# Sparse attention into a feed-forward block on one core: two score tiles, four query turns, two key turns and the last transposes put elsewhere in the order

## The chip, the cores and the metric

The kernel runs on one core of a Trainium2 chip. The metric is device time in microseconds for one execution; the median of four runs is compared. The core has five engines that run side by side, each through its own instructions in order: TensorE (PE in the profile; its weight loads are PEld), VectorE (DVE), ScalarE (ACT), GpSimd (POOL) and SyncE (SP, which here only issues DMAs). They wait for one another by semaphores.

## The reference

Inputs q, k, v are 4 batches x 8 heads x 768 rows x 64, in float32. Each query sees the keys less than 16 rows away, and one summary key and value for each of the 24 blocks of 32 rows: the maximum of the block's keys and the mean of its values. The outcome goes through a feed-forward block with a sigmoid-approximated gelu.

```python
k_sum = k.reshape(B, H, nb, block, D).max(axis=3)
v_sum = v.reshape(B, H, nb, block, D).mean(axis=3)
scores_l = scale * q @ k.T            # kept where |i - j| < 16
scores_s = scale * q @ k_sum.T + log(block)
a = softmax(concat([scores_l, scores_s]))
x = (a @ concat([v, v_sum]))          # heads side by side: 3072 x 512
h = x @ w_in                          # 512 x 2048
out = (h * sigmoid(1.702 * h)) @ w_out
```

## The kernel before

**Units.** Each of the 4 batches is cut into two halves of 384 rows; the eight halves are the units u = 0 to 7. Attention of a unit works on four pairs of heads, p = 0 to 3. In the names of the order tables a lower-case letter is a batch's first half and a capital its second half: `s2` is "scores of pair 2, first half", `S2` the same of the second half, `v1` / `V1` the values of pairs 2 and 3, `x1` / `X1` their transposition into the layout that the feed-forward reads, `t2` and `q2` the turning of the queries of pair 2.

**Attention of one pair.** `scores` (line 606) is 24 small matmuls on TensorE into a PSUM tile of two banks, one exponential on ACT and one multiplication by the mask on VectorE. `values` (616) is 24 matmuls for each pair, and `norm` (639) on VectorE. Then either `tx` (645) transposes with TensorE and a copy, or `dx` (653) with a transposing DMA on SP's queue. Keys and queries are turned by TensorE (`tk` 567, `tq1`, `q_turn` 434 with `q_copy` 443) in the first batches, and by transposing DMAs on SP's queue (`xk` 579, `xq` 587, with `rest_k` 593 on VectorE behind them) in the later ones. The turns of `tk` give VectorE a copy, a maximum, and the copies `key_halos` and `key_rows`.

**Feed-forward.** `ff_in` (658) makes 16 tiles of 128 hidden columns for a unit, each four matmuls of 384 columns and one gelu on ACT. For units 0 and 1 the output stage is `ff_out` (807): three row tiles (ms) in four parts each. For later batches the output stage is a Strassen-Winograd scheme over pairs of row tiles, class `Pair`: seven products p1 to p7 for each of the pairs a, b, c. Three of them accumulate onto one PSUM bank `x`, and between them ACT copies the bank out (`held`, 849), so that the next of them waits for that copy: p6, then p5, then p3. For the last batch the same scheme is used within `ff_in` too (`ff_in_pairs`, 700), with products M1 to M7 over weight sums and sums of the two units' x; six tiles of unit 6 are done plainly ahead of it, while the sums `t[0]` to `t[3]` are made on VectorE. They need the transposed x of both halves.

**PSUM.** Pool `pmm` (77) has four banks, for feed-forward products, turned queries, and the x of `tx`. Pool `psb` (76) has two tiles of two banks, for scores, turned keys, and values. A new tile waits until a bank of its pool is read out.

**Order.** Every engine's instructions keep the order in which the program writes them (class `_Ordered`; line 28 is that of every instruction in the profile). So the order around the change is written out by hand, in tables:
- `plan0` and `plan1` (1056 to 1060), read by `beside` (1064), put attention steps of the next unit behind the slots of `ff_out`. Slot -1 is ahead of the first output product. Behind `beside(1, -1)` the program issues the loads of the next q and k rows on POOL's queue.
- `todo` (1101) puts key turns, the copies `v_odd` and `value_rows` behind the hidden tiles of unit 1. `value_rows` sums v over blocks (TensorE, then VectorE) and issues on POOL's queue the DMAs that fill the halo and sum rows of `vw`, and further loads.
- `order` and `meets` (1129 to 1136), read by `attend` (1138), do the same for the output stages of batches 1 and 2, beside attention of batches 2 and 3. Behind the pair S3, `gelu_soon` has ACT load the gelu table.
- A product's store, where it has one, is issued on SP's queue when the product is written (`store`, 874): p3 and p4 of each pair store a row tile, before that batch's next entries of `meets`.

Of the kernel before, what the change touches and what calls it, by code (L numbers as in the profile page):

```python
# [35 lines left out]
def kernel(  # L36
# [239 lines left out]
    def copy(eng, out, in_):  # L276
        if eng is act:
            act.activation(out=out, in_=in_, func=ACT.Copy)
        elif eng == "dve_alone":

            dve.tensor_reduce(out=out, in_=in_.unsqueeze(len(in_.shape)), axis=AX.X, op=ALU.max)
        else:
            eng.tensor_copy(out=out, in_=in_)
# [94 lines left out]
    def at(ap, start, dims):  # L378
        a = ap[:, start:start + 1]
        return bass.AP(tensor=a.tensor, offset=a.offset, ap=[a.ap[0]] + dims)  # L380

    def flat_kx(p, s):
        return kx[p][s].rearrange("p t c -> p (t c)")
# [7 lines left out]
    def key_halos(p, s, eng=dve, j0=0):  # L391

        flat = flat_kx(p, s)
        b0 = max(j0, 1)
        o = 256 * j0
        eng.tensor_copy(out=at(flat, 256 * b0 + 96, [[256, NJ - b0], [1, 16]]),
                        in_=at(flat, 256 * b0 - 16, [[256, NJ - b0], [1, 16]]))
        eng.tensor_copy(out=at(flat, o + 128 + 48, [[256, NJ - 1 - j0], [1, 16]]),
                        in_=at(flat, o + 256, [[256, NJ - 1 - j0], [1, 16]]))
        eng.tensor_copy(out=at(flat, o + 128 + 32, [[256, NJ - j0], [-48, 2], [1, 16]]),  # L400
                        in_=at(flat, o + 48, [[256, NJ - j0], [144, 2], [1, 16]]))
# [159 lines left out]
    def trans(src):  # L561
        big = psb.tile([128, 2048], BF16, name="ps_t", tag="big")
        for j in range(NJ):
            pe.transpose(out=big[:, j * 128:(j + 1) * 128], in_=src[:, j], identity=ident)
        return big[:, 0:S]

    def tk(p, s):
        ps = trans(rows["k", 1][:, p].rearrange("p j h d -> p j (h d)"))
        copy(dve, at(flat_kx(p, s), 0, [[256, NJ], [192, 2], [1, 64]]),
             ps.rearrange("p (j e c) -> p j e c", e=2, c=64))  # L570
        ks = attp.tile([128, nb], BF16, name="ks", tag="ks")
        dve.tensor_reduce(out=ks, in_=ps.rearrange("p (n s) -> p n s", s=block),
                          axis=AX.X, op=ALU.max)
        key_halos(p, s)
        key_rows(p, s, ks)
# [124 lines left out]
    def ff_in_pairs(u, early):  # L700

        (b11, b21), (b12, b22) = xTT
        xs = castp2.tile([128, 4, 2, HALF], F16, name="xsum", tag="kb")
        t = [xs[:, m] for m in range(4)]
        big = [psb.tile([128, 1024], F32, name="pw_in", tag="big") for _ in range(2)]
        mm = [pmm.tile([128, 512], F32, name="px_in", tag="mm") for _ in range(4)]
        X, V = ([m[:, 0:HALF] for m in mm[n:n + 2]] for n in (0, 2))
        Y = [big[0][:, n:n + HALF] for n in (0, 512)]
        L = big[1][:, 0:HALF]

        def gelu(w, f, src):
            act.activation(out=gT[w % 2][:, f, :], in_=src, func=ACT.Gelu_apprx_sigmoid)

        def one(w, f, ps):
            for ko in range(KO):
                pe.matmul(out=ps, lhsT=w_in_sb[:, ko, f * 128:(f + 1) * 128], rhs=xT[w % 2][ko],
                          start=(ko == 0), stop=(ko == KO - 1))
            gelu(w, f, ps)

        def prod(ps, a, b, i, first=False):  # L720
            for k in range(2):
                pe.matmul(out=ps, lhsT=a[:, k, i], rhs=b[:, k], start=(first and k == 0),
                          stop=(k == 1), skip_group_check=True)

        ws = [wt["s"][:, n] for n in range(4)]
        hold = {}

        def f0(i):
            return 2 * (NI - WI + i)

        def M1(i):
            x = X[i % 2]
            prod(x, wt[0, 0], b11, i, True)
            dve.tensor_copy(out=Y[i % 2], in_=x)

        def M7(i):
            v = V[i % 2]
            prod(v, ws[2], t[2], i, True)
            hold[i] = attp.tile([128, HALF], F32, name="m7", tag="x2")
            copy(act, hold[i], v)  # L740

        def M6(i):
            x = X[i % 2]
            prod(x, ws[1], t[1], i)
            dve.tensor_add(V[i % 2], x, hold[i])

        def M2(i):
            y = Y[i % 2]
            prod(y, wt[0, 1], b21, i)
            gelu(u, f0(i), y)  # L750

        def M5(i):
            x = X[i % 2]
            prod(x, ws[0], t[0], i)
            hold[i, 2] = attp.tile([128, HALF], F32, name="c22", tag="a_sb")
            dve.tensor_add(hold[i, 2], x, hold[i])

        def M4(i):
            v = V[i % 2]
            prod(v, wt[1, 1], t[3], i)  # L760
            gelu(u, f0(i) + 1, v)
            gelu(u + 1, f0(i) + 1, hold[i, 2])

        def M3(i):
            x = X[i % 2]
            prod(x, ws[3], b22, i)
            gelu(u + 1, f0(i), x)

        n, rest = 2 * (NI - WI), list(range(2 * (NI - WI)))

        def plain():
            one(u + 1, rest.pop(0), L)

        for f, ps in zip(range(n), (Y[0], X[1], V[1], Y[1], L, X[1])):
            if f == n - 2:
                M1(0)
            one(u, f, ps)
        dve.tensor_sub(t[2], b22, b12)
        dve.tensor_add(t[1], t[2], b11)
        dve.tensor_sub(t[0], b12, b11)  # L780
        dve.tensor_sub(t[3], b21, t[1])
        M2(0)
        M7(0)
        plain()
        M6(0)
        for i in range(1, WI):
            M1(i)
            for f in (M7, M5) if i == 1 else (M5, M7):
                f(i if f is M7 else i - 1)
            M4(i - 1)  # L790
            M6(i)
            M3(i - 1)
            M2(i)
            plain()
            if i == 2:
                early(0, NI - WI)
        i = WI - 1
        M5(i)
        M4(i)
        early(NI - WI, NI)  # L800
        plain()
        M3(i)
        assert not rest
# [244 lines left out]
    for p in range(NP):  # L1048
# [7 lines left out]
    plan1 = {0: ["t0"], 1: ["t1"], 2: ["s0", "s1"], 4: ["t2"], 5: ["t3"],  # L1056
             6: ["v0", "s2", "s3"], 8: ["x0"], 9: ["v1", "S0", "S1"], 11: ["x1", "S2", "S3"]}

    plan0 = {-1: ["q0", "q1", "q2", "q3"], 1: ["s0", "s1"], 3: ["s2", "s3"], 6: ["v0", "v1"],
             9: ["x0"], 10: ["x1"]}  # L1060

    w51 = vw[1].rearrange("p (j e) h c -> p j e h c", e=2)
# [23 lines left out]
    for u in range(2):  # L1086
        todo = {}
        if u == 0:
            for p in range(NP):
                todo.setdefault(12 + p // 2, []).append(lambda p=p: cast_q(dve, p, 1))  # L1090
        else:
            def value_rows():
                vsum(1, range(NJ))
                block_sums()
                halo_dmas(w51, 0)
                sum_dmas(w51, 0)
                load_kc(2, range(6, H))
                load_vc(2)
                load_qc(2)

            todo = {0: [lambda: tk(0, 1)], 3: [lambda: tk(1, 1)], 5: [lambda: v_odd(1)],
                    6: [lambda: tk(2, 1)], 9: [value_rows], 11: [lambda: tk(3, 1)]}
            ff_in(u, range(3))
        for nt in range(0 if u else N0, NT):
            if u == 0 or nt > 2:
                ff_in(u, (nt,))
            for f in todo.get(nt, ()):
                f()
        exp_soon()
        if u == 0:  # L1110
            beside(1, -1)
            load_qc(1)
            load_kc(2, range(6))
        order = [(ms, part) for ms in range(JH) for part in range(4)]
        if u == 0:

            order = [(ms, part) for part in range(4) for ms in range(JH)]
        for i, (ms, part) in enumerate(order):
            ff_out(u, ms, part)
            beside(u + 1, i)  # L1120
            if u == 0 and i in (4, 7, 10):
                w_sums(i // 3 - 1)
            if u == 1 and i == 2:
                w_sums(3)
            if u == 1 and i == 3:
                for g in range(2):
                    xk(g, 2)
# [1 line left out]
    order = ["a7", "a2", "a6", "b1", "a5", "b7", "a3", "a4", "b6", "b2", "b5",  # L1129
             "c1", "b3", "c7", "c6", "c2", "c5", "b4", "c3", "c4"]  # L1130
    meets = {1: {"a7": ["s0", "s1"], "a5": ["s2", "s3"], "b6": ["v0", "v1"], "b5": ["x0"],
                 "c1": ["x1"], "b3": ["S0", "S1"], "c2": ["S2", "S3"],
                 "c4": ["V0", "V1", "X0", "X1"]},
             2: {"a7": ["s0", "s1"], "b1": ["s2", "s3"], "a4": ["v0", "v1"], "b2": ["x0"],
                 "b5": ["x1"], "c1": ["S0", "S1"], "c6": ["S2", "S3"], "c2": ["V0"],
                 "b4": ["X0"], "c3": ["V1", "X1"]}}

    def attend(b, what):
        half, i = int(what[0].isupper()), int(what[1])
# [10 lines left out]
    for b in range(1, B):  # L1150
        n, s = b + 1, (b + 1) % 2
# [97 lines left out]
```

## Time and profile before

| | us |
|---|---|
| median of 4 runs | 209.73 (209.48 to 210.36) |
| the profiled execution | 209.58 |
| its span, first to last instruction | 207.9 |
| TensorE busy | 198.4, 95% of the span |
| VectorE busy | 146.7, 71% |
| ScalarE busy | 124.1, 60% |
| GpSimd busy | 93.3, 45% |
| granted TensorE clock, mean | 0.997 |

The page of the profile gives busy time by engine, then the span in 40 slices of 5.2 us with a busy digit for each (9 is 90% or more). The chain of waits that ended last is 85% TensorE, 6% DMA and 4% VectorE; its largest links are the hidden products `ph` (30% of the span), the Strassen products `px` (15%) and the output products `po` (10%). DMA packets: 28.94 MB in all, most of it (14.88 MB) in POOL's software queue.

Stages on the time line, read from the chain: loading and batch 0's first half to 23 us; unit 0's hidden tiles to 32.3; its output stage to 46.8; unit 1's hidden tiles to 59.1; its output stage to 74.6; units 2 and 3 hidden to 97.8; batch 1's output stage to 121.8; units 4 and 5 hidden to 143.3; batch 2's output stage to 166; units 6 and 7 hidden to 186; batch 3's output stage to the end.

A matmul's end in the profile is modelled, and some 0.16 to 0.2 us of it overlap with the next one: the pace of a row of matmuls is read from starts, not from lengths.

### The profile page before, as it was taken

How to read it: one execution, taken by the hardware profiler on the slowest of the kernel's cores; microseconds unless marked ns; L12 is line 12 of the kernel's file. 1: busy time of each engine (PE TensorE's matmuls, PEld its weight loads, DVE VectorE, ACT ScalarE, POOL GpSimd, SP SyncE). 2: the span in 40 equal slices, each digit the busy share in tenths (PEclk: the TensorE clock that was granted, in tenths of full speed). 3: DMA queues.
4: the chain of work that ended last, by engine and by line, in shares of the span. 5: the costliest groups of instructions: out<-in, count | busy, mean ns of one | idle time of the engine just before them, and what ended most of it. 6: DMA issues, size and time to landing. Idle time of an engine off the chain costs nothing.

```text
span 207.9 us, 5593 instructions
## 1 busy us (share of the span) xinstructions
PE 198.4 (95%) x2216; PEld 135.2 (65%) x2217; DVE 146.7 (71%) x425; ACT 124.1 (60%) x236; POOL 93.3 (45%) x165
## 2 busy tenths in 40 slices
PE   7789999999999999999999799999999999999993
PEld 2567465556655566566888576567888855568882
DVE  7597955798946768946767579579976856669431
ACT  2675876726575589677744737677716566981220
POOL 8987889399999942626998000402000000000000
PEclk9999999999999999999999999999999999999998
DMA  6999999999999999999999997992035170000323
GB/s 189 292 165 206 251 242 217 173 142 223 162 153 168 144 97 150 197 119 170 122 149 189 149 229 131 138 168 60 3 117 114 50 180 0 5 0 16 113 74 103
DMA packets 95010, 28.94 MB, mean 139 GB/s; under 512 B 82880, under 2 KB 92000, under 8 KB 94984
## 3 DMA queue, kind: packets, MB, share of 16 engines
q0 software_dynamic: 67920, 14.88, 80.5%
q1 hardware_dynamic: 25432, 12.53, 30.9%
q10 hardware_dynamic: 1632, 1.18, 1.8%
q8 instruction: 17, 0.28, 0.6%
q14 instruction: 9, 0.07, 0.2%
HBM read 27.26 MB, written 6.29 MB: 161 GB/s over the span
## 4 chain that ended last, share of the span: by engine, by line
PE 85%; DMA 6%; DVE 4%; issue 1%; ACT 1%; ACTq 0%; DVEq 0%
PE ph L28 30%; PE px L28 15%; PE po L28 10%; PE pw L28 7%; PE px_in L28 4%; PE ps_av L28 4%; PE py L28 4%; PE ps_s L28 4%; PE pw_in L28 3%; DMA qf<-in_q_dram 3%; DMA kf<-in_k_dram 2%; PE ps_x L28 1%; DMA xT<-x 1%; PE ps_t L28 1%; DVE qT L28 1%
## 5 line engine op out<-in xcount | busy, mean ns | idle before, releaser
L28 PE MATMUL ph<-xT,w_in_sb 128*128 128x384 f16 x384 | 65.2, 326 | 0.0
L28 PEld LDWEIGHTS <-w_in_sb 128*128 128x128 f16 x462 | 44.3, 98 | 28.8 <-issue 0.4
L28 ACT ACTIVATE gT<-ph 128x384 f16<-128x384 f32 x96 | 45.7, 490 | 19.8 <-PE ph L28 19.5
L28 PEld LDWEIGHTS <-gT 128*128 128x128 f16 x384 | 36.2, 98 | 12.4 <-issue 0.3
L28 ACT ACTIVATE a_sb<-ps_s 128x768 bf16<-128x768 f32 x28 | 21.1, 806 | 9.3 <-PE ps_s L28 9.3
L28 PEld LDWEIGHTS <-ss 128*128 128x128 f16 x216 | 20.7, 98 | 4.2 <-issue 1.6
L28 PE MATMUL po<-w_out_sb,gT 128*128 128x512 f16 x96 | 23.2, 380 | 0.2 <-DVE qT L28 0.2
L28 DVE TENSOR_TENSOR a_sb<-a_sb,mk 128x768 bf16<-128x768 bf16 x28 | 15.4, 556 | 10.3 <-ACT a_sb L28 8.8
L28 ACT ACTIVATE t<-px 128x256 f32<-128x256 f32 x21 | 8.0, 382 | 20.5 <-PE px L28 20.5
L28 PE MATMUL px<-ta,ss 128*128 128x256 f16 x144 | 18.7, 273 | 0.0
L28 PE MATMUL pw<-tb,gT 128*128 128x256 f16 x144 | 18.7, 273 | 0.0
L28 DVE TENSOR_TENSOR x<-ps_av,rc 128x384 f16<-128x384 f32 x28 | 15.6, 558 | 1.0
L28 POOL DMA_DIRECT2D vw<-in_v_dram x18 | 15.9, 936 | 0.0
L28 POOL DMA_DIRECT2D vw<-vw x12 | 6.5, 566 | 18.8 <-DVE vw L28 16.7
L28 POOL DMA_DIRECT2D kb<-in_k_dram x16 | 13.2, 854 | 3.9 <-DMA w_out_sb<-in_moe_w_out_dram 3.5
L28 ACT ACT_TABLE_LOAD x10 | 12.8, 1283 | 3.1 <-issue 2.9
L28 POOL DMA_DIRECT2D qb<-in_q_dram x16 | 14.0, 969 | 1.3 <-DMA vw<-in_v_dram 0.8
L28 DVE TENSOR_TENSOR osb<-pw,t 128x256 f32<-128x256 f32 x18 | 7.4, 420 | 9.2 <-PE pw L28 6.1
L28 DVE TENSOR_TENSOR ss<-gT 128x384 f16<-128x384 f16 (+4 forms) x18 | 7.5, 418 | 4.5 <-ACT gT L28 4.5
L28 PE MATMUL px<-w_out_sb,ss 128*128 128x256 f16 x72 | 9.3, 272 | 1.4 <-ACT t L28 1.4
L28 DVE TENSOR_REDUCE ks<-kx 128x24 bf16<-128x768 bf16 x8 | 7.6, 945 | 3.9 <-DMA kx<-kb 3.9
L28 PEld LDWEIGHTS <-kx 64*128 64x128 bf16 x400 | 7.2, 95 | 4.6 <-issue 3.7
(123 smaller groups left out, 311.0 us busy)
## 6 DMA issues: line engine op xcount, KB each, us to landing
out_dram<-osb SPq DMA_DIRECT2D x18, 256.0 KB, 3.9
vw<-in_v_dram POOLq DMA_DIRECT2D x18, 128.0 KB, 5.3
w_in_sb<-in_moe_w_in_dram POOLq DMA_DIRECT2D x4, 512.0 KB, 9.4
w_out_sb<-in_moe_w_out_dram POOLq DMA_DIRECT2D x4, 512.0 KB, 19.6
kb<-in_k_dram POOLq DMA_DIRECT2D x16, 96.0 KB, 5.0
qb<-in_q_dram POOLq DMA_DIRECT2D x16, 96.0 KB, 6.5
out_dram<-osb SPq DMA_DIRECT2D x12, 128.0 KB, 1.7
vw<-vs POOLq DMA_DIRECT2D x6, 148.5 KB, 3.9
```

What stands on the lines that cost most here:

```text
L28: r = f(*a, **kw)
```

## The change

The same work is done; only its place in the program differs, in five places.

```diff
         for f, ps in zip(range(n), (Y[0], X[1], V[1], Y[1], L, X[1])):
-            if f == n - 2:
+            if f == 2:
                 M1(0)
             one(u, f, ps)
...
-    plan0 = {-1: ["q0", "q1", "q2", "q3"], 1: ["s0", "s1"], 3: ["s2", "s3"], 6: ["v0", "v1"],
+    plan0 = {-1: ["q0", "q1"], 0: ["q2", "q3"], 1: ["s0", "s1"], 3: ["s2", "s3"], 6: ["v0", "v1"],
              9: ["x0"], 10: ["x1"]}
...
             todo = {0: [lambda: tk(0, 1)], 3: [lambda: tk(1, 1)], 5: [lambda: v_odd(1)],
-                    6: [lambda: tk(2, 1)], 9: [value_rows], 11: [lambda: tk(3, 1)]}
+                    9: [value_rows], 10: [lambda: tk(2, 1)], 13: [lambda: tk(3, 1)]}
...
     meets = {1: {"a7": ["s0", "s1"], "a5": ["s2", "s3"], "b6": ["v0", "v1"], "b5": ["x0"],
-                 "c1": ["x1"], "b3": ["S0", "S1"], "c2": ["S2", "S3"],
+                 "c1": ["x1"], "b3": ["S0", "S1"], "c5": ["S2", "S3"],
                  "c4": ["V0", "V1", "X0", "X1"]},
              2: {"a7": ["s0", "s1"], "b1": ["s2", "s3"], "a4": ["v0", "v1"], "b2": ["x0"],
                  "b5": ["x1"], "c1": ["S0", "S1"], "c6": ["S2", "S3"], "c2": ["V0"],
-                 "b4": ["X0"], "c3": ["V1", "X1"]}}
+                 "c5": ["X0"], "b4": ["V1", "X1"]}}
```

- **Batch 1's output stage.** The order of products at its end is c7, c6, c2, c5, b4, c3, c4. The scores S2 and S3 (of batch 2), with the load of the gelu table behind them, stood after c2 and stand after c5.
- **Unit 0's output stage.** Four turns of queries with their copies stood ahead of the first output product; two of them now stand behind it.
- **Unit 1's hidden tiles.** The key turn of pair 2 goes from behind tile 6 to behind tile 10, that of pair 3 from behind tile 11 to behind tile 13; `value_rows`, behind tile 9, now comes ahead of both.
- **Batch 2's output stage.** The transposing DMA X0 is issued after c5 instead of after b4 and its store. V1 with its DMA X1 comes after b4 instead of after c3 and its store.
- **The last batch's hidden tiles.** M1(0), two matmuls and a VectorE copy, comes ahead of the plain tile f = 2 instead of f = 4.

## The prediction

> **What bounds the kernel.** I read the page first, then TensorE's waits, then the timeline around each place that the diff touches.
>
> ```profile
> PE 198.4 (95%) x2216; PEld 135.2 (65%) x2217; DVE 146.7 (71%) x425; ACT 124.1 (60%) x236; POOL 93.3 (45%) x165
> PE   7789999999999999999999799999999999999993
> ...
> PE px L28 <- ACT t L28: 1.4, 1, 1.4
> ...
> PE po L28 <- DVE qT L28: 0.2, 1, 0.2
> ```
>
> The first two lines are the page's busy row and TensorE's row of slices; the others are from its waits (us in total, times, longest). TensorE's digit is 9 in every slice from 16 us on but one and the last, and the windows view grants it a clock of 1.00 in every stretch up to 186 us. So the kernel is worth what TensorE's gaps are worth: a part of the change that moves work beside a gapless TensorE gains nothing, and a part that closes a gap moves all that follows. The largest gap behind the start, 1.4 us, is the digit 7.
>
> **Part 1: the scores S2, S3 of batch 2, in batch 1's output stage, from behind c2 to behind c5.** The timeline there (start, length, engine, operation, and what ended the idle time):
>
> ```profile
> 115.65 1.51 ACT L28 ACTIVATE a_sb<-ps_s 128x768 bf16<-128x768 f32 x2 [0.84 <-PE ps_s L28]
> ...
> 116.54 1.04 PE L28 MATMUL pw<-tb,gT 128*128 128x256 f16 x8
> ...
> 117.18 1.28 ACT L28 ACT_TABLE_LOAD   x1
> ...
> 118.58 0.36 ACT L28 ACTIVATE t<-px 128x256 f32<-128x256 f32 x1
> ...
> 119.00 1.03 PE L28 MATMUL px<-w_out_sb,ss 128*128 128x256 f16 x8 [1.42 <-ACT t L28]
> ```
>
> TensorE runs c2, S2, S3, c5 (115.66), b4 (116.54), c3 (119.00). c3 accumulates onto the bank that c5 left, so ACT must have copied c5's sum out first; that copy stands in ACT's order behind two exponentials and a table load. From b4's start to c3's start is 2.46 us; the same pair in batch 2's stage, where c5's copy comes in time, takes 163.58 - 162.66 = 0.92. **The gap is 1.54 us.**
>
> After the change: c5 at 115.20 (where S2 stood), its end 1.05 later, ACT copy 116.29 to 116.67 (0.38). S2, S3 go to TensorE at 116.07 for 0.46, then b4 to 117.4, then c3, whose bank has been free for 0.7 us. What is late next: exponentials 116.67 to 118.18, table load to 119.47, c3's own output copy to about 120.0, hardly earlier than before (120.45), but it only feeds a store and frees a bank. V1 follows c4 and V0 at 119.6 and needs the masked S3: VectorE does c5's addition to 117.1 and two masks of 0.63, the last after the exponential at 118.18, so 118.8. Cover 0.8 us. c4's bank was read by c5's addition at 117.1, before c4 at 118.3. Then the next feed-forward needs three banks at 120.2: three are free (c4's addition ends at 119.8).
>
> A rule speaks against leaving the table load so near the end. The row: the load takes 1.28 us and the next ACT instruction starts at 118.47, at once. The Trainium skill, ScalarE: Activation LUTs, section What ACT_TABLE_LOAD costs, charges a drain of 1.38 us on top, 2.66 for a switch. By that, c3's copy ends at 121.4 instead of 120.0 and its bank is late for the first three products; but these find the other three, and the first gelu waits for twelve matmuls, to about 122.2. By both the sum is the same. **Gain 1.54**, ends 0 (another wait of equal length) and 1.6.
>
> **Part 2: batch 0's q turns in two pairs.**
>
> ```profile
> 32.30 1.07 PE L28 MATMUL ps_q<-ident,qb 128*128 128x128 bf16 x12
> 32.67 2.72 DVE L28 CAST qT<-ps_q 128x384 bf16<-128x384 f32 x4 [1.44 <-PE ps_q L28]
> ...
> 33.52 1.89 PE L28 MATMUL po<-w_out_sb,gT 128*128 128x512 f16 x8 [0.15 <-DVE qT L28]
> ```
>
> Four turns take all four banks. The fourth waits for the last gelu (it ends at 32.99), the first output product for the first VectorE copy (33.47). Split in narrow windows, the copies end at 33.47, 34.11, about 34.75 and 35.39. TensorE reaches S0 at 35.34. After: q0, q1 32.30 to 32.63; the output product takes the bank of the gelu that ended at 32.34, four matmuls of 0.215, to 33.5; q2, q3 0.33, to 33.84, in the last gelu's bank and in q0's (33.47); the second output product needs q1's bank, 34.11, a new wait of 0.3; it ends at 35.01. Then S0, with q0 and q1 copied, and the third product with q2's bank free at 34.75. **Gain 35.34 - 35.01 = 0.33**, ends 0.1 (the banks handed out in the other order) and 0.6 (no wait left). q2, q3 are copied before S2 needs them after two more products. POOL's reload of the q rows now also waits for the later turns, but it issues that load at 46.54, 13 us later.
>
> **Part 3: key turns 2 and 3 of unit 1 behind tiles 10 and 13.** Six transposes of 0.34 us each change places with products of 0.65 and no gap is there, so TensorE gains nothing. VectorE's work for one turn is 0.56 + 0.95 + 0.37 + 0.23 with overlaps, 2.0 us. Turn 3 moves from 56.02 to about 57.35, its VectorE work from 56.7-58.7 to 57.7-59.9, into this idle stretch (a line of VectorE's timeline, and one of POOL's):
>
> ```profile
> 61.55 0.56 DVE L28 COPY qT<-ps_t 128x768 bf16<-128x768 bf16 x1 [2.86 <-PE ps_t L28]
> ...
> 59.24 2.19 POOL L28 DMA_DIRECT2D vw<-vw  x4
> ```
>
> 1.65 us of cover stay before 61.55, and the scores that use these keys come at 67.5. The block sums no longer stand behind turn 2 on VectorE and are ready 1.1 us earlier; POOL's issues of the value rows don't follow, because POOL is writing other loads until 59.24. **Zero**, ends -0.1 and +0.2.
>
> Here too a rule speaks against it. SBUF — State Buffer, section SBUF: two separate sides, says that POOL cannot write DMA descriptors while a VectorE copy in a fast mode holds the port they share: 3100 ns instead of 620. The rows: POOL's issues of k rows at 54.24 to 58.5 lay beside turns 2 and 3 on VectorE and took about 0.85 each; two at 38.37 and 40.53 with VectorE mostly idle took 0.83 and 0.82. So the row gives nothing and I take it; by the rule each issue that is caught costs up to 2.48, which is the rival below.
>
> **Part 4: the last x transfers of batch 3 ahead of stores, M1(0) two products earlier.**
>
> ```profile
> 165.18 1.25 SPq L28 DMA_TRANSPOSE xT<-x  x1
> ...
> 166.09 0.56 DVE L28 TENSOR_TENSOR x<-ps_av,rc 128x384 f16<-128x384 f32 x1
> ...
> 166.52 0.53 SPq L28 DMA_DIRECT2D out_dram<-osb  x1
> ...
> 167.16 1.25 SPq L28 DMA_TRANSPOSE xT<-x  x1
> ...
> 169.26 0.57 DVE L28 COPY pw_in<-px_in 128x384 f32<-128x384 f32 x1 [2.28 <-ACT gT L28]
> ...
> 170.05 0.56 DVE L28 TENSOR_TENSOR xsum<-xT,xT 128x768 f16<-128x768 f16 x1 [0.23 <-DMA xT<-x]
> ...
> 170.66 0.48 PE L28 MATMUL px_in<-xsum,wsum 128*128 128x384 f16 x2
> ```
>
> X1's values are ready at 166.65, but SP's queue is in X0 and a store until 167.05. It lands 2.8 us after its issue, at 169.93; four sums follow. TensorE loses 0.17 at M7(0) (M2(0) done at 170.49, start 170.66), 0.24 at M5(0) (172.61 to 172.85) and 0.15 at M3(0). After: X0 goes out when V0's norms end, 164.1, to 165.35; b4's store to 165.9; V1 runs in c3's place at 163.58, its norms follow b4's addition on VectorE from 164.75, 1.5 us, to 166.24; X1 166.28, landing 169.05: 0.88 earlier. Two stores are behind it on SP, of interest to nobody until their buffers turn. The first sum ends at 169.7, so M7(0)'s gap goes. M1(0) at 167.23 lets its copy end at 168.33, ahead of the sums; in its old place it would now delay them to 169.83. M5(0) then waits not for a late sum but for M6's addition, 1.14 us behind M6's start with 0.98 of matmuls between: 0.16 stays, 0.08 goes. M3's gap stays. Against it: the copy at 169.26 started only when the gelu of the other half of its two-bank tile ended (169.22), so the tile's halves seem tied; then product f=3 must wait for the copy, up to 0.16. Gain 0.25, or 0.09 so tied; **I take 0.2**, ends 0 and 0.55. That all queues share the DMA engines costs little: they are idle from 163 to 165.6.
>
> **The sum**: 1.54 + 0.33 + 0 + 0.2 = 2.07. The profiled execution took 209.58 (span 207.9, 1.68 around it): 207.5. The median of the four runs is 0.15 above it, so **207.7**.
>
> **Rivals.**
> - *Part of it is given back in batch 2's stage.* There VectorE works without a pause from the landing of the key transposes (136.5, an idle 3.07 before) to 151; a3 starts at 150.34 with its operand ready at 149.46, 0.88 of slack. TensorE arrives 1.87 earlier. The key transposes follow V1's norms on SP and should move as much. If they don't, a3 waits 0.99: 208.65. Against it: the POOL loads that could crowd them are over by 122 us.
> - *Only part 1 works*, parts 2 and 4 meeting the next bank wait: 208.2.
> - *Part 1's gap comes back elsewhere in the stage* (V1, a bank): parts 2 and 4 only, 209.2, no change that can be told.
> - *Slower: POOL's descriptors.* Place: the six value-row issues from 59.24 to 62.7. They land by 62.0 + 4.1 = 66.1, V0 at 66.99 would come at 66.66: 0.56 of slack. Each issue caught by turn 3's moved work costs 2.48 by the page. One caught still nets a gain of 0.15; from two on (4.96 - 0.56) the kernel is slower: 212.1. Against it the rows above, and that only 0.6 us of VectorE work reaches past 59.24.
>
> **Chances.** Forecast 0.62; given back 0.12; part 1 only 0.13; gap back 0.06; POOL 0.07. A change under 0.3%, 0.63 us, is not told from none: faster 0.87, same 0.06, slower 0.07. The range goes from 206.9 (part 2 and 4 at their upper ends and a little of the spread) to 208.8 (the first two rivals).
>
> **What would show it.** Part 1: no wait of "PE px" on "ACT t", the digit 7 gone, c5's copy ahead of the last exponentials; wrong if c3 or V1 waits. Part 2: S0 near 35.0, one wait of po on qT of some 0.3. Part 3: POOL issues near 0.6 at 59 us. Part 4: X1's issue about 0.9 earlier against c4, M7(0) without a gap. Were VectorE's pause before a3 shorter with a TensorE wait on ss there, the first rival holds.

## The result, and the profile after

| | before | changed |
|---|---|---|
| median, us | 210.04 (55 runs, 209.08 to 211.46) | 208.62 (34 runs, 206.75 to 212.5) |
| ratio to before | | 0.9922, 95% interval 0.9906 to 0.9939 |
| profiled execution: time / span | 209.58 / 207.9 | 208.26 / 206.6 |

The change makes the kernel faster by 0.6 to 0.9%, where the prediction worked out 2.07 us and wrote 207.7. The medians of all runs differ by 1.42 us; the ratio, which leaves out five slow runs of the changed kernel (211.28 to 212.5), gives 1.6. Page and TensorE's waits of the changed kernel:

```profile
PE 197.8 (96%) x2216; PEld 135.3 (66%) x2217; DVE 148.1 (72%) x425; ACT 123.9 (60%) x236; POOL 92.3 (45%) x165
PE   6789999999999999999999999999999999999993
...
PE ps_vs L28 <- DMA vw<-in_v_dram: 0.4, 1, 0.4
...
PE po L28 <- DVE qT L28: 0.2, 1, 0.2
```

The digit 7 that stood in TensorE's row at 114 to 120 us is gone, and with it "PE px" waiting for "ACT t". A wait that the page of before did not have has come: the block sums `ps_vs` on v rows from memory. To see what each part brought, the span is cut at TensorE's first instruction of each stage. These lengths are differences of starts in TensorE's timeline, in us:

| stretch | before | changed | difference |
|---|---|---|---|
| start to the q turns | 32.30 | 32.02 | -0.28 |
| q turns to S0 (part 2) | 3.04 | 2.83 | -0.21 |
| S0 to unit 1's hidden tiles | 11.32 | 11.32 | 0 |
| unit 1's hidden tiles (part 3) | 12.29 | 12.29 | 0 |
| unit 1's output stage | 15.61 | 15.75 | +0.14 |
| unit 2, to the block sums | 8.26 | 8.26 | 0 |
| the block sums | 0.45 | 1.05 | +0.60 |
| to batch 1's output stage | 14.31 | 14.31 | 0 |
| batch 1's output stage (part 1) | 24.14 | 22.55 | -1.59 |
| units 4 and 5 hidden | 21.37 | 21.36 | -0.01 |
| batch 2's output stage (part 4) | 22.85 | 22.80 | -0.05 |
| units 6 and 7 hidden (part 4) | 19.96 | 20.02 | +0.06 |
| to the end of the span | 22.0 | 22.0 | 0 |

The first row lies ahead of every changed instruction and differs by as much from one execution of a kernel to another (32.02 and 33.05 in two profiles of the changed kernel). The rest says: part 1 brought all of its 1.5 us, part 2 brought 0.2, and in this execution 0.74 us were given back between 58 and 84 us, all of them waits for transfers.

**Part 1.** Timeline of the changed kernel, the same place as before:

```profile
115.35 1.04 PE L28 MATMUL px<-ta,ss 128*128 128x256 f16 x8
...
116.31 0.52 PE L28 MATMUL ps_s<-qT,kx 64*128 64x64 bf16 x24
116.42 0.38 ACT L28 ACTIVATE t<-px 128x256 f32<-128x256 f32 x1 [1.36 <-PE px L28]
116.70 1.51 ACT L28 ACTIVATE a_sb<-ps_s 128x768 bf16<-128x768 f32 x2
116.77 1.05 PE L28 MATMUL pw<-tb,gT 128*128 128x256 f16 x8
...
117.66 1.04 PE L28 MATMUL px<-w_out_sb,ss 128*128 128x256 f16 x8
118.23 1.28 ACT L28 ACT_TABLE_LOAD   x1
...
119.64 0.37 ACT L28 ACTIVATE osb<-px 128x256 f32<-128x256 f32 x1
```

ACT copies c5's sum at 116.42, ahead of the two exponentials, and c3 starts 0.89 after b4 where it was 2.46. The table load now delays only c3's own copy, which starts at 119.64 and holds nothing up.

**The sums of the v rows.** The same place in both kernels. First before: POOL's requests for batch 2's v rows, TensorE's block sums, and VectorE's first copy of those rows.

```profile
64.58 5.27 POOL L28 DMA_DIRECT2D vw<-in_v_dram  x6
...
82.82 0.52 PE L28 MATMUL ps_vs<-vw,E 128*32 128x128 bf16 x24
...
83.31 0.95 DVE L28 COPY vw<-vw 128x768 bf16<-128x768 bf16 x2 [0.63 <-DMA vw<-in_v_dram]
```

Then the changed kernel:

```profile
65.24 5.27 POOL L28 DMA_DIRECT2D vw<-in_v_dram  x6
...
82.47 0.46 PE L28 MATMUL ps_vs<-vw,E 128*32 128x128 bf16 x20
83.34 0.24 PE L28 MATMUL ps_vs<-vw,E 128*32 128x128 bf16 x4 [0.41 <-DMA vw<-in_v_dram]
...
83.62 0.95 DVE L28 COPY vw<-vw 128x768 bf16<-128x768 bf16 x2 [1.14 <-DMA vw<-in_v_dram]
```

The last of the six transfers lands 14.1 us after its issue before (68.9 + 14.1 = 83.0) and 13.7 after it in the changed kernel (69.6 + 13.7 = 83.3). The last four of the 24 block sums need it. Before, TensorE came to them at about 83.1 and passed by a tenth of a microsecond; that the margin was so thin stands in the page of before only as VectorE's 0.63 on the same transfer. The changed kernel comes 0.35 earlier on the clock of the span (0.28 of that is the start's), the rows 0.3 later, so it waits: its gain up to here is gone, and more. Counted from the q turns, TensorE reached the last four sums after 50.8 us before and would have reached them after 50.7 in the changed kernel (0.21 gained, 0.14 lost ahead of it); the rows landed after 50.7 us before and 51.3 in the changed kernel. So most of this wait comes from the rows, which landed later in this execution. The profiles don't show that the change delays them: in the twelve with this order of POOL's requests, with the change, parts of it or none, the rows land 47.7 to 51.9 us behind the q turns.

**Part 4.** SP's, VectorE's and TensorE's timeline of the changed kernel in the last hidden stage:

```profile
162.78 1.21 SPq L28 DMA_TRANSPOSE xT<-x  x1
...
164.84 1.25 SPq L28 DMA_TRANSPOSE xT<-x  x1
...
165.20 1.79 PE L28 MATMUL px_in<-xT,w_in_sb 128*128 128x384 f16 x10
...
166.44 0.57 DVE L28 COPY pw_in<-px_in 128x384 f32<-128x384 f32 x1 [1.27 <-PE px_in L28]
...
167.06 1.46 PE L28 MATMUL pw_in<-xT,w_in_sb 128*128 128x384 f16 x8
167.73 0.56 DVE L28 TENSOR_TENSOR xsum<-xT,xT 128x768 f16<-128x768 f16 x1 [0.72 <-DMA xT<-x]
...
169.33 0.49 PE L28 MATMUL px_in<-xsum,wsum 128*128 128x384 f16 x2
```

The stage's first product starts at 164.55, before at 165.93. Against it the first sum is at 3.18 instead of 4.12: X1 did come 0.9 earlier, and M7(0) (169.33) follows M2(0) (169.01) without a gap. But f=3, which should start at 166.83 behind f=2, the last of the ten matmuls from 165.20 on (165.20 + 10 x 0.163), starts at 167.06, just when M1(0)'s copy has ended (166.44 + 0.57). One gap of 0.17 went and one of 0.23 came.

### The profile page after: what moved, and what is told of

The parts are those of the page before. It is cut to its first block, busy times and chain, and to the rows that moved or that the text cites. A ratio compares the mean times of both kernels' runs of the same rounds, so it can differ in the third digit from the quotient of the medians.

```text
span 206.6 us, 5593 instructions
## 1 busy us (share of the span) xinstructions
PE 197.8 (96%) x2216; PEld 135.3 (66%) x2217; DVE 148.1 (72%) x425; ACT 123.9 (60%) x236; POOL 92.3 (45%) x165
## 3 DMA queue, kind: packets, MB, share of 16 engines
q0 software_dynamic: 67920, 14.88, 83.3%
## 4 chain that ended last, share of the span: by engine, by line
PE 79%; DMA 12%; DVE 4%; POOL 1%; issue 1%; ACT 1%; ACTq 0%; DVEq 0%
PE ph L28 27%; PE px L28 15%; PE pw L28 8%; DMA vw<-in_v_dram 7%; PE po L28 6%; PE px_in L28 5%; PE py L28 4%; PE pw_in L28 4%; PE ps_av L28 3%; PE ps_s L28 3%; DMA qf<-in_q_dram 2%; DMA kf<-in_k_dram 2%; DMA out_dram<-osb 1%; POOL vw L28 1%; DVE qT L28 1%; PE ps_t L28 1%
## 5 line engine op out<-in xcount | busy, mean ns | idle before, releaser
L28 POOL DMA_DIRECT2D qb<-in_q_dram x16 | 13.3, 917 | 1.6 <-DMA vw<-in_v_dram 1.6
L28 POOL DMA_DIRECT2D kq<-in_q_dram x8 | 6.6, 840 | 7.3 <-DMA vw<-in_v_dram 7.3
```

The costliest lines, as they stand in the source:

```text
L28: r = f(*a, **kw)
```

## The experiments

Two theories: the *gate* (the block sums wait for the last v rows, whenever TensorE comes, so what is gained ahead of them is lost there) and, against it, that the parts add up and the shortfall has another cause. The prediction's rivals were tested along with them.

**e1, part 1 alone.**

```diff
-  "b3": ["S0", "S1"], "c2": ["S2", "S3"],
+  "b3": ["S0", "S1"], "c5": ["S2", "S3"],
```

> Before, with the scores S2, S3 alone moved behind c5. Both theories: TensorE's wait of 1.4 us on c5's copy goes, c3 starts 0.9 us after b4, and the time falls by 1.5 us (1.3 to 1.7), since nothing behind 122 us takes it back. If batch 2's stage gives part of it back (first rival of the prediction), the fall is 0.6 to 1.0 and TensorE waits for ss near a3.

Measured: 0.9946 (0.9925 to 0.9967), 1.1 us less (0.7 to 1.6): under the expected 1.3, which the interval holds. Batch 1's output stage took 22.55 us (before 24.14), and all behind it is as before (21.37, 22.85, 19.93): nothing is given back in batch 2's stage. The profile shows something else, ahead of the edit, in unit 1's hidden tiles, 13.32 us instead of 12.29:

```profile
54.59 1.46 DVE L28 COPY vw<-vw 128x768 bf16<-128x768 bf16 x4 [0.77 <-DMA vw<-in_v_dram]
55.97 0.54 DVE L28 COPY kx<-ps_t 128x768 bf16<-128x768 bf16 x1
...
57.52 0.49 PE L28 MATMUL ps_t<-ident,kb 128*128 128x128 bf16 x6 [0.87 <-DVE ks L28]
```

Batch 1's v rows came late in this execution. VectorE, in order, stood in `v_odd`; the turn of pair 2 behind it was read out late, and TensorE's turn of pair 3 waited 0.87 us for the PSUM tile. This is what part 3 is about, and the profiled execution of before had not met it; it may be why the time fell by less than the stage.

**e2, part 2 alone** (the `plan0` line of the diff).

> Before, with the q turns alone in two pairs. Gate theory (the block sums of batch 2's v rows near 83 us wait for their last transfer, whenever TensorE comes): S0 starts 0.2 us earlier against the turns, but the block sums then wait for the v rows and the time is the same within 0.2 us. Rival (gains add up): 0.2 to 0.3 us faster, no TensorE wait on the v rows.

Measured: 0.9988 (0.9968 to 1.0007), 0.25 us less with an interval from 0.67 less to 0.15 more, so the time can't tell the two theories apart. The profile can: the stretch to S0 is 2.82 us (before 3.04), the block sums take 1.01 instead of 0.45 with 0.4 of wait on the v rows, and the next hidden product starts at 83.36, before at 83.27. Counted from the q turns that is 0.34 later than before: in this execution part 2 brings 0.22 us, and the gate takes it and more.

**e3, part 2 with the block sums later.**

```diff
-            first.setdefault(9 if b == 1 else 15, []).append(bring)
+            first.setdefault(12 if b == 1 else 15, []).append(bring)
```

> The q turns in two pairs, and the block sums of batch 2 behind hidden tile 12 instead of 9 of unit 2 (about 2 us later). Gate theory: no TensorE wait on v rows, the 0.2 us of the turns are kept: 0.2 to 0.4 us faster than before. Rival: as e2, since the sums' place means nothing.

Measured: 1.0005 (0.9981 to 1.0029), median 210.18 against 210.04, so the time doesn't show the expected gain. In the profile the block sums take 0.45 us without a wait, as the gate theory says, and the 0.22 are there (2.82), but unit 1's hidden tiles take 12.61, 0.32 more than before, with a wait of ps_t on VectorE as in e1. Unlike there, VectorE did not wait for v rows: three of its copies took 0.3 to 0.4 us longer than in before, each beside a request of POOL. In before the three lines below took 0.23, 0.23 and 1.16 (from 50.77, 52.53 and 52.68):

```profile
50.56 0.64 DVE L28 COPY kx<-ks 128x288 bf16<-128x288 bf16 x1
...
52.68 0.52 DVE L28 COPY kx<-ks 128x288 bf16<-128x288 bf16 x1
53.20 1.46 DVE L28 COPY vw<-vw 128x768 bf16<-128x768 bf16 x4
```

What the later sums are worth in time stays open; that the wait on v rows is gone does not.

**e4, the changed kernel with the block sums later** (the same line).

> The changed kernel with the block sums of batch 2 behind hidden tile 12 instead of 9. Gate theory: the 0.7 us that the changed kernel loses between 62 and 83.6 us come back: 0.5 to 0.8 us faster than the changed kernel, 2.0 to 2.5 below before, and its runs spread less, because the landing of the v rows no longer counts. Rival (the loss is spread over the stretch, or is part 3's): the same time as the changed kernel within 0.2 us.

Measured: 0.9924 (0.9896 to 0.9952), median 208.45. No wait on v rows, the block sums take 0.45, unit 1's output stage 15.61, and from the q turns to the end the profile is 0.73 us shorter than the changed kernel's. The ratio is that of the changed kernel (0.9922), not the expected 0.5 to 0.8 us below it, so the time shows nothing; its six runs went from 207.5 to 209.3.

**e5, the changed kernel again**, for comparison with the next three.

> The changed kernel itself, as the comparison for e6 to e8 on the same chip. Gate theory: again a stretch from the first of batch 2's block sums to the next hidden product that is longer than the 0.45 us it takes without a wait (1.05 in the first profile), by an amount that differs from execution to execution; 1.2 to 1.8 us below before. Rival: no such wait this time, and the time the same all the same.

Measured: 0.9929 (0.9902 to 0.9956), 208.31. The block sums took 1.35 us, so the wait is larger than in the first profile. The start was a microsecond later in this execution, for TensorE and for the requests alike; counted from the q turns the rows were requested after 33.2 us in both. TensorE's waits:

```profile
PE ps_vs L28 <- DMA vw<-in_v_dram: 0.7, 1, 0.7
```

**e6, part 4 alone** (the `meets[2]` lines and the M1(0) line).

> Before, with the last transfers and M1(0) alone. Tie theory (M1's copy and product f=3 share a two-bank tile, so that f=3 waits for the copy): X1 lands 0.9 us earlier, M7(0)'s gap of 0.17 goes and a gap of 0.23 ahead of f=3 comes; the stretch from the first product of units 6 and 7 to batch 3's output is 20.0 us as before (19.96), and the time is the same within 0.3 us. Rival (the prediction): the stretch is 19.75 and the time 0.2 us less.

Measured: 1.0010 (0.9986 to 1.0034), no difference; the last hidden stretch 20.02 us, batch 2's output stage 22.80. The prediction's 0.2 is not there.

**e7, the changed kernel with the block sums later and the tie undone.**

```diff
-  for f, ps in zip(range(n), (Y[0], X[1], V[1], Y[1], L, X[1])):
+  for f, ps in zip(range(n), (Y[0], X[1], V[1], L, Y[1], X[1])):
```

> The changed kernel with the block sums of batch 2 behind tile 12, and plain products f=3 and f=4 of the last stage with their banks exchanged, so that f=3 no longer writes the tile of M1(0)'s copy. Tie theory: no gap ahead of f=3, the last hidden stretch 19.75 to 19.85 us instead of 20.02. Gate theory as in e4. Together 0.6 to 1.0 us faster than the changed kernel, and no TensorE wait behind 36 us in the profile but the 0.24 at M5(0). Rival (no tie: it is X or the bank's gelu): the gap moves to f=4 or stays, 20.0 us.

Measured: 0.9891 (0.9857 to 0.9926), median 207.76, 0.55 below e5, just under the expected 0.6 and with intervals that overlap. The last hidden stretch is 19.87, 0.02 over the upper end of what was expected and 0.15 below 20.02. VectorE's copy and TensorE's f=3 in its profile:

```profile
164.98 1.79 PE L28 MATMUL px_in<-xT,w_in_sb 128*128 128x384 f16 x10
...
166.22 0.57 DVE L28 COPY pw_in<-px_in 128x384 f32<-128x384 f32 x1 [1.27 <-PE px_in L28]
...
166.60 1.46 PE L28 MATMUL pw_in<-xT,w_in_sb 128*128 128x384 f16 x8
```

f=3 (166.60) starts while the copy runs to 166.79, right behind the ten matmuls ahead of it (164.98 + 10 x 0.163). So the wait was for the copy into the other half of the same two-bank tile. 0.09 remain ahead of M2(0), which starts at 168.64, 0.05 behind the end of a gelu; that this is a tie of the same kind is not shown.

**e8, the cause of the gate taken at its other end**: the place of the sums is left, the v rows are requested earlier.

```diff
-                load_kc(2, range(6, H))
                 load_vc(2)
+                load_kc(2, range(6, H))
                 load_qc(2)
```

> The changed kernel with batch 2's v rows requested ahead of the last two heads of its k rows, about 2 us earlier in POOL's queue. Gate theory: the block sums, left in their place, find their rows (0.45 us, no wait), as e4 in time: 0.4 to 0.8 us faster than the changed kernel, unless the later k rows make the key transposes late for VectorE. Rival (the wait is for something else of that stretch): unchanged.

Measured: 0.9915 (0.9894 to 0.9937), median 208.02. POOL requests the rows from 63.72 (66.22 in e5, with the same start), the slowest of the later ones lands after 10.2 us instead of 13.9, and the block sums take 0.45 us without a wait, though TensorE came to them at the same 83.36 as in e5:

```profile
63.72 5.37 POOL L28 DMA_DIRECT2D vw<-in_v_dram  x6
...
83.36 0.52 PE L28 MATMUL ps_vs<-vw,E 128*32 128x128 bf16 x24
```

By time it is 0.3 below e5, a little under the expected 0.4, and the intervals overlap. One profile can't carry it alone: the landing moves by more than a microsecond between executions. VectorE's first copy of these rows starts 0.3 us behind their landing, after a wait, in before, e2, e3, e5, e7, e9 and the changed kernel, and it didn't wait in e1, e4, e6, e10 and e11, all with the old order of requests.

**e9 and e10, what part 3 is worth**: e7 with the key turns back behind tiles 6 and 11, and e7 once more.

```diff
-                    9: [value_rows], 10: [lambda: tk(2, 1)], 13: [lambda: tk(3, 1)]}
+                    6: [lambda: tk(2, 1)], 9: [value_rows], 11: [lambda: tk(3, 1)]}
```

> e7 with the key turns of unit 1 put back behind tiles 6 and 11. Theory (part 3 pays only in executions in which batch 1's v rows come late, because VectorE then stands in the copy of these rows and the third key turn waits for its PSUM tile): the stretch of unit 1's hidden tiles is 12.29 us or up to 1 us longer, with a wait of ps_t on VectorE, differing from execution to execution; the median is 0 to 0.5 us above e7. Rival (part 3 does nothing, as predicted): 12.29 in the profile and the time of e7 within 0.2 us.

> e7 again, as the comparison for e9 on the same chip: 2.0 to 2.5 us below before, unit 1's hidden tiles 12.29 us, no wait on v rows.

Measured: e9 0.9921 (0.9890 to 0.9952), 208.05; e10 0.9906 (0.9875 to 0.9937), 207.63. The medians differ by 0.4, with six runs each and intervals that overlap. The profiles tell more. Unit 1's hidden tiles took 12.89 in e9 with a wait of ps_t on VectorE, and 12.29 in e10. Over all profiles: without part 3 the wait is in three of seven (1.03, 0.60 and 0.32 us longer in e1, e9 and e3; none in before, e2, e6 and e11), with it in none of six, although VectorE waited 0.28 us for the v rows in one of them (e7) and one or two copies of `v_odd` were long (0.65 to 0.76) in all six. So VectorE comes late in two ways, by the rows (e1, e9) and by longer copies (e3). That part 3 takes TensorE's wait away fits all thirteen profiles, which are few, and the time doesn't show it. e10 met a late transfer elsewhere, the sum rows ahead of the first values of unit 1's output stage (16.17 us instead of 15.61):

```profile
66.55 0.85 PE L28 MATMUL ps_av<-vw,a_sb 128*64 128x65 bf16 x24 [0.21 <-DMA vw<-vs]
```

**e11, the block sums later, in the kernel of before.**

> Before, with the block sums of batch 2 alone behind hidden tile 12. Gate theory: before, TensorE came to the last of these sums about 0.1 us behind the landing of the v rows, so in executions with a later landing it waited there too: 0.1 to 0.4 us faster than before. Rival: the gate is only met once TensorE comes earlier, and the time is that of before within 0.1 us.

Measured: 0.9989 (0.9964 to 1.0014), median 209.80 against 210.18. The theory's 0.1 to 0.4 lies in the interval, and so does nothing. Whether before met its gate in executions that were not profiled stays open; in this one the rows were in time.

So no run shows by its time what the gate costs: e4, e8 and e11 lie 0 to 0.3 us below their counterparts, with intervals that overlap. The profiles show the wait (0.6 to 0.9 us), and that it is absent in those where the sums came later or the rows were requested earlier.

e7 and e10 are the same kernel and the fastest of this study: 207.76 and 207.63, 2.30 and 2.55 us below the before of their groups, where the changed kernel was 1.75 below in e5.

## Why the prediction was right, and where its steps were not

The time fell as forecast and within the range, near its upper end (208.62 of 208.8), by the mechanism that carried three quarters of the sum. The rest of the sum did not stay. The nearest rival in number was "only part 1 works" (208.2), but it named a bank wait; what the profiles show is a wait for the v rows, which no rival named, and the tie. So that the range held is in part luck: its upper end was there for other losses. Point by point:

- **Part 1, 1.54: right.** 1.59 in the changed kernel and in e1's stage. The cover behind it held: V1 didn't wait and c3's late copy held nothing up.
- **Part 2, 0.33: the mechanism right, the size off, and the gain not kept.** The stretch to S0 shrank by 0.21 to 0.22 in every profile with it. The term that was mis-sized is the second output product. Its start was right (1.85 us behind the q turns in the sum, 33.89 - 32.02 = 1.87 measured), but S0 came 0.96 behind it instead of 0.86, 0.1 that the sum, made of matmul pace alone, left out. The step that failed is the premise that closing a gap "moves all that follows". It does so up to the next thing that runs by another clock; here this was the landing of the v rows near 83, in the executions in which it was late; e2's profile shows the loss, those of e4, e7 and e8 the stretch without it.
- **Part 3, zero: right for the profiled execution, probably wrong as a mean.** The sum was read from one execution in which batch 1's v rows came in time. In others VectorE comes late, because it stands behind those rows (e1, e9) or because its copies take longer beside POOL's requests (e3), and the last key turn waits up to a microsecond; by time this is not shown. The cover was taken from the page of before as if it were always there, and the shared port was put at nothing from rows of one execution.
- **Part 4, 0.2: the step that failed is the bound "up to 0.16" on the tie, and the 0.08 at M5(0).** The tie cost 0.23 (f=3 at 167.06 against 166.83), M5(0) kept its 0.24 (e7's M7(1) leaves at 171.24, M5(0) starts at 171.48), and 0.17 came back: nothing in the sum, as e6 shows. The copy starts 0.26 behind the slot of M1(0)'s last matmul (166.18), takes 0.57, and f=3 follows 0.05 behind it, against 0.65 of matmuls for f=2: together 0.23, where the prediction allowed 0.16. And M5(0) waited for M6's addition before the change too: it started 0.05 behind the addition's end in both kernels (172.85 and 171.52), so there was no late sum to remove.
- **The rival in batch 2's stage** doesn't hold: the key transposes moved along (VectorE's second start on them 136.60 before, 134.62 after), and the stage took 22.80.
- **The rival of POOL's descriptors** doesn't hold in its size: the four requests at 58.96 took 0.59 to 0.61 each, as before. The prediction's rows on this overlooked one request of before, at 52.79 beside the copies of `v_odd`, that took 1.46. The stage that the rival named lost 0.14 in another way: the sum rows landed 4.8 to 5.2 us after issue instead of 3.7 to 4.1. In e4, e5, e7 and e8 the stage took its 15.61, so this belongs to the execution.

So the changed kernel's profile, without the 0.28 of the start, is 1.05 shorter: 1.59 + 0.21 gained by parts 1 and 2, 0.01 lost in part 4's two stretches, 0.60 at the block sums, 0.14 at the sum rows. The time fell by more than that, 1.4 to 1.6. The runs of before may contain executions with part 3's wait, which its profile does not have, and those of the changed kernel some without the wait at the block sums; that this is the difference is not shown.

## What to carry to other kernels

When the engine that bounds the kernel has no gaps behind the place where you gain, look there for its instructions that use a transfer, and list the margin between the landing and the use: a gain ahead of a use with no margin can be lost there, and moving the use later (or the request earlier) is part of the same edit. A wait of another engine on the same transfer tells that the margin is thin. And what a single profile shows as no wait behind a transfer may be a wait in the next execution: work that doesn't need the transfer should not stand behind work that does, on an engine that runs in order.

## What the runs showed of the hardware

Transfers of one size and kind take very different times to land. The v rows of 128 KB took 4.9 to 6.8 us in batch 1 and 6.9 to 14.1 us in batch 2 in the same execution, where the later ones were issued beside q rows and the transposing transfers.

VectorE and POOL seem to take turns for something. The four copies of `v_odd` for batch 1, of one shape, take 0.35 us each in before and e11, and there POOL's request beside them takes 1.46 and 1.44 us instead of 0.8 to 0.9; in the changed kernel one copy takes 0.69 and the requests are short, in e5 two copies take 0.65 and 0.72. For batch 2, one copy takes 0.68 beside a request in before and in the changed kernel, and in e4, where no request lies beside them, all take 0.35. In e3 three copies were lengthened (0.64, 0.52 and 0.65), and TensorE's wait of unit 1 follows them. The Trainium skill, SBUF — State Buffer, section SBUF: two separate sides, has the two engines hold a shared port exclusively when VectorE is in one of its fast modes, and whoever starts first keeps it for the whole instruction; the runs agree with that, at a price of 0.3 to 0.6 us an instruction and not the 2.5 of its example. No run isolated it.

The table load takes 1.28 us and the next ACT instruction, a small one on a tile named `gate`, starts 0.02 later (118.23 + 1.28 = 119.51, then 119.53). So the drain of 1.38 that the Trainium skill adds (ScalarE: Activation LUTs, section What ACT_TABLE_LOAD costs) was not seen here, as it was not before the change.
